# One batch of scores per head pair in a fused state-space and attention kernel: four PSUM banks at once, projections run further ahead, more of the out-projection inside attention

## The chip, the cores and the metric

The kernel runs on one core of a Trainium2 chip. The metric is the device time of one execution in microseconds (us). A core has five engines with a queue each: TensorE (PE in the profile; PEld is its weight load), VectorE (DVE), ScalarE (ACT), GpSimd (POOL) and SyncE (SP), which here issues nearly all DMAs. Matmuls write to PSUM[...].

## What is computed

Two independent parts share one input length T = 2048 and are written side by side. Part A is a diagonal state-space layer; the change leaves it alone. Part B is attention over 64 segments of 32 tokens, each with 8 memory rows in front (32 heads of 128):

```python
for s in range(n_seg):
    h = concat([mem, x[:, s*32:(s+1)*32]])           # 8 + 32 rows
    q, k, v = (einsum('btd,dhe->bhte', h, W) for W in (Wq, Wk, Wv))
    p = softmax(where(mask, q @ k^T * 128**-0.5, -1e9))
    o = einsum('bhte,hed->btd', p @ v, Wo)
    mem = o[:, :8];  outs.append(o[:, 8:])
```

The kernel doesn't follow the recurrence over `mem` one segment after another: it uses a guess of the memory rows for all segments at once, gathers numbers that bound the error, and at the end a flag decides whether a general path must run. In the runs here it isn't run.

## The kernel before

**Stages.** First come the values of part B and part A's scan, then part A's output product (`stage2`), up to about 465 us of the profile. Then follows the stage that the change is about: attention over 16 *head pairs* `hp` (two heads each), from about 465 to 990 us. The last stage is the rest of the out-projection, from 990 us to the end.

**Projections.** `proj` is a generator that makes q and k (transposed) of one head pair in 18 *blocks*: for each of four column quarters q hh0, q hh1, k hh0, k hh1, eight matmuls of 480 columns each (L581), and then two tail blocks (one for q, one for k) of 16 matmuls of 136 columns (L592). Each block accumulates in one of two PSUM banks called P. VectorE copies q blocks and both tails to SBUF (L77, tiles b_q and b_k), ScalarE copies k blocks (L75). In the second quarter ScalarE also squares the weights (`norm`, L564), and the next pair's weights are loaded (`load_wqk`, L554). q and k have two sets of buffers, one per parity of `hp`.

**Units of attention.** A pair has nine units: eight ordinary ones (0 to 7, two blocks of 128 tokens each) and the memory unit, number 8 (`NU`), for the first segment. The order is 0, 1, 2, 3, 4, 5, 8, 6, 7. `att_front` of a unit makes its probabilities, `att_back` uses them two units later:

- Ahead of units 0 and 4, `scores` runs 32 small matmuls (L637), two banks S of 16. They use half of TensorE's columns each, so two of them lie side by side, in 64 rows of the output. ScalarE takes the exponential of each bank (L642, b_e, with a sum in accE). Units 0 to 3 read token columns up to the middle, so these scores need 12 of the pair's 18 blocks; the later ones need all.
- GpSimd multiplies each unit's b_e with the causal mask: two instructions, a *mask pair* (L653, b_mx, four buffers). The memory unit has its own score (L659), exp (L661) and mask (L663, b_ms).
- `att_back` multiplies the masked probabilities with v: four matmuls of 129 columns (L694) into one of two *O pairs* of banks; VectorE adds a memory term (L696, b_s from b_u) and takes reciprocals (L698); GpSimd scales (L702, b_ot). After units 3 and 7 SP writes b_ot to DRAM (b_os, L709 and L710). For the memory unit it is two matmuls (L673), then b_om (L679).

So PSUM holds P, P (projections), S, S (scores and small sums), and O in two pairs.

**The order of the work** on TensorE is written by hand in `kernel_main`: a number of blocks is made ahead of the first unit (`done = 12`), and after each unit blocks are made until `done` is `12 + 2 * (n + 1)`, so two per unit. When the 288 blocks of all pairs are done, each further unit takes two pieces of four matmuls from `early`, a part of the out-projection (`op_some`, L750): tiles 0 and 1, output half 0, three of four head groups, accumulated in the two P banks. A pool framework places semaphores, and a planner orders the instructions of the other engines; each engine's order is then fixed.

**Loads.** b_v and b_u (the values and memory terms of half a pair) have three buffers each; at unit 2 the next pair's first half is loaded, at unit 6 its second (`load_v` L605, `load_u` L618). Four stages of `v_mem` (the values of the memory rows: 32 matmuls L483, DMAs, the certificate term b_ct L498 and its sums L510) go between units 3 to 6 of the first pairs.

**After attention** five transposing loads of b_os (`load_o`, L737, b_ol) are issued on SP. TensorE meanwhile does tiles 2 and 3, half 0 (48 matmuls, banks S), then all four tiles of half 1 (96 matmuls, both O pairs), all with the three head groups that are there. Then the fourth group (64 matmuls), and then tiles 4 to 15. `check` (a generator) loads b_omd transposed (L794), and computes the flag beside tiles 4 to 7.

Of the kernel before, what the change touches and what calls it, by code (L numbers as in the profile page):

```python
# [2 lines left out]

# [6 lines left out]
BF16 = mybir.dt.bfloat16  # L10
I32 = mybir.dt.int32
ACT = mybir.ActivationFunctionType
# [28 lines left out]
UPH = NU + 1  # L41
# [252 lines left out]
class PartB:  # L294
# [219 lines left out]
    def qk_init(self, pool):  # L514
        V, G = self.k.V, self.k.G
        self.qk = []
        for i in range(2):
            self.qk.append([pool.tile([128, 2, QW], BF16, name=f"b_{n}{i}", bufs=1) for n in "qk"])
        self.vmst = []
        for i in range(2):  # L520
            t = pool.tile([128, 4, 128], BF16, name=f"b_vmst{i}", bufs=1)
            V.memset(t[:, :, NM:128], 0.0)
            self.vmst.append(t)
        self.ct = pool.tile([128, 2, 256], BF16, name="b_ct", bufs=1)
        V.memset(self.ct[:], 0.0)
        self.vb, self.ub = [], []
        for i in range(3):
            t = pool.tile([128, NU, VW], BF16, name=f"b_v{i}", bufs=1)
            u = pool.tile([128, NU, VW], BF16, name=f"b_u{i}", bufs=1)
            for c in (0, VW - 1):  # L530
                G.memset(t[:, :, c:c + 1], 1.0)
                G.memset(u[:, :, c:c + 1], float(M))
            self.vb.append(t)
            self.ub.append(u)
        self.vs = pool.tile([128, 2, VW], BF16, name="b_vs", bufs=1)
        G.memset(self.vs[:], 0.0)
        for c in (0, VW - 1):
            G.memset(self.vs[:, :, c:c + 1], 1.0)
        self.ms = []
        self.mx, self.es = [], {}  # L540
        for i in range(4):
            t = pool.tile([128, 4, 128], BF16, name=f"b_mx{i}", bufs=1)
            G.memset(t[:], 0.0)
            self.mx.append(t)
        for i in range(2):
            t = pool.tile([128, 2, 128], BF16, name=f"b_ms{i}", bufs=1)
            G.memset(t[:], 0.0)
            self.ms.append(t)
# [76 lines left out]
        k.SP.dma_start(dst(0, M), self.vt[hb][0:M, :].rearrange("p (h n) -> p h n", h=2))  # L625
        k.SP.dma_start(dst(M, L), self.vx[hb][0:SEG, :].rearrange("p (h n) -> p h n", h=2))

    def scores(self, hp, u0):

        k = self.k  # L630
        qt, kt = self.qk[hp % 2]
        for v in range(2):
            s = k.ps("S")
            for j in range(8):
                g = M + (2 * (u0 + 2 * v + j // 4) + j // 2 % 2) * 128
                for r in (0, 64):
                    k.tc.keep_in_program_order(k.PE.matmul(  # L637
                        s[r:r + 64, j * 64:j * 64 + 64], kt[:, j % 2, g + r:g + r + 64], qt[:, j % 2, g + r:g + r + 64],
                        start=True, stop=True))
            e = self.p3.tile([128, 512], BF16, name="b_e", bufs=3)  # L640
            i = hp * UPH + u0 + v
            k.S.activation(e[:], s[:], ACT.Exp, scale=float(E) ** -0.5, accum_out=self.accE[:, i:i + 1])  # L642
            self.es[u0 + 2 * v], self.es[u0 + 2 * v + 1] = (e[:, 256 * a:256 * a + 256] for a in range(2))

    def att_front(self, hp, u):
        k = self.k; PE = k.PE
        if u < NU:
            if u % 4 == 0:
                self.scores(hp, u)
            m = self.mx[u % 4]  # L650
            e = self.es.pop(u).rearrange("p (j q) -> p j q", j=4)
            for r in (slice(0, 64), slice(64, 128)):
                k.G.tensor_tensor(m[r, :, r], e[r], k.maskX[r, r].unsqueeze(1).to_broadcast([64, 4, 64]), ALU.mult)  # L653
            return m
        qt, kt = self.qk[hp % 2]
        s = k.ps("S")
        i = hp * UPH + u
        for hh in range(2):
            PE.matmul(s[:, hh * L:(hh + 1) * L], kt[:, hh, 0:128], qt[:, hh, 0:L], start=True, stop=True)  # L659
        e = self.p3.tile([128, 2 * L], BF16, name="b_es", bufs=1)  # L660
        k.S.activation(e[:], s[:, 0:2 * L], ACT.Exp, scale=float(E) ** -0.5, accum_out=self.accE[:, i:i + 1])  # L661
        m = self.ms[hp % 2]
        k.G.tensor_tensor(m[:, :, 0:L], e[:].rearrange("p (j q) -> p j q", j=2), k.maskM[:].unsqueeze(1).to_broadcast([128, 2, L]), ALU.mult)  # L663
        return m
# [45 lines left out]
            k.SP.dma_start(os[1024 * half + 128 * (1 - half):1024 * half + 1024, cs].rearrange("(g p) n -> p g n", p=128), ot[:, 1 - half:NU, :])  # L710

    def attention(self):
        units = [(hp, u) for hp in range(HP) for u in (0, 1, 2, 3, 4, 5, NU, 6, 7)]
        pend = []
        for n, (hp, u) in enumerate(units):
            if u == 2:
                self.load_v(2 * hp + 2)
                self.load_u(2 * hp + 2)
            if u == 3 and hp % 2 == 0:
                self.load_vs(hp // 2)  # L720
            if u == 6:
                self.load_v(2 * hp + 3)
                self.load_u(2 * hp + 3)
            pend.append((hp, u, self.att_front(hp, u)))
            if len(pend) > 2:
                self.att_back(*pend.pop(0))
            yield hp, u
        for p in pend:
            self.att_back(*p)
            yield HP, 0  # L730
# [58 lines left out]
    def check(self):  # L789
        k = self.k; V, S, PE = k.V, k.S, k.PE  # L790
        pool = self.p4

        omT = pool.tile([128, H, MT], BF16, name="c_om", bufs=1)
        k.SP.dma_start(omT[:], self.omd[:, :], transpose=True)  # L794
        a = pool.tile([128, H], FP32, name="c_a", bufs=1)
        d = pool.tile([128, H, M], FP32, name="c_d", bufs=1)
        w = pool.tile([128, M], FP32, name="c_w", bufs=1)
# [29 lines left out]
        for i, (acc, limit, op) in enumerate(((self.accE, RANGE, ALU.is_le), (self.rall, RANGE, ALU.is_le), (self.cert, 0.0, ALU.is_ge))):  # L827
            n = acc.shape[1]
# [104 lines left out]
def kernel_main(tc, A_x, A_Lre, A_Lim, A_Bre, A_Bim, A_Cre, A_Cim, A_logdt, A_Dskip, B_x, B_mem0, B_Wq, B_Wk, B_Wv, B_Wo, out,  # L933
                force=False, dbg=None):
    with ExitStack() as ctx:
        k = K(tc, ctx)
# [3 lines left out]
        a = PartA(k, A_x, A_Lre, A_Lim, A_Bre, A_Bim, A_Cre, A_Cim, A_logdt, A_Dskip, out)  # L940
        b = PartB(k, B_x, B_mem0, B_Wq, B_Wk, B_Wv, B_Wo, out)
# [10 lines left out]
        with pool("p1", "right") as p1:  # L952
# [35 lines left out]
            v = values()  # L988
            done = 0
# [16 lines left out]
            for n in range(PC * NB):  # L1006
# [7 lines left out]
                want = 20 + 4 * (n + 1) if n < 4 else 36 + (92 * (n - 3) + 27) // 28  # L1014
# [33 lines left out]
        with pool("p2", "right") as p2:  # L1048
            g = b.guess()
# [15 lines left out]
        with pool("p3", "right") as p3:  # L1065
            b.p3 = p3
            b.qk_init(p3)
            pr, at = b.proj(), b.attention()
            vms = [b.v_mem(hb) for hb in range(HB)]
            for hb in range(2):  # L1070
                next(vms[hb])
            vm = vms[0]
            done = 12
            next(vm)
            b.load_v(0)
            for i in range(done):
                next(pr)
                if i in (0, 2):
                    next(vm)
                if i == 2:  # L1080
                    b.load_u(0)
                    b.load_v(1)
                if i == 5:
                    b.load_u(1)
            b.wo0, b.acc = [], {}
            early = b.op_some([(0, 0), (1, 0)], range(3), "P", 2)
            for n, (hp, u) in enumerate(at):
                if u in (3, 5, 6) and hp < 7:
                    next(vms[hp + 1])
                if u == 4 and hp < 6:  # L1090
                    next(vms[hp + 2])
                if u == 4 and 8 <= hp < 12:
                    w = k.w8((8, 512), "wo0")
                    k.SP.dma_start(w, b.Wo[:, 8 * (hp - 8):8 * (hp - 7), 0:512])
                    b.wo0.append(w)
                if u == 6 and hp in (4, 8, 12):
                    b.load_o(0, hp // 4 - 1)
                want = min(18 * HP, 12 + 2 * (n + 1))
                if done == want:
                    for _ in range(2):  # L1100
                        next(early, None)
                while done < want:
                    next(pr)
                    done += 1
                    if done == 18 * HP:
                        w1 = xep.tile([128, KC, XP], BF16, name="b_xe")
                        b.wo1 = w1[:].rearrange("p c n -> p (c n)")[:, 0:H * 512].rearrange("p (h n) -> p h n", h=H)
                        k.SP.dma_start(b.wo1, b.Wo[:, :, 512:D])
            for _ in early:
                pass  # L1110

        with pool("olb", "right", 5) as olb, pool("p4", "right") as p4:
            b.p4 = p4
            b.olp[1] = olb
            for i in range(5):
                b.load_o(*divmod(i + 3, 4))
            for _ in b.op_some([(2, 0), (3, 0)], range(3), "S"):
                pass
            for _ in b.op_some([(0, 1), (1, 1), (2, 1), (3, 1)], range(3), "O"):
                pass  # L1120
            for half in range(2):
                for t in range(4):
                    b.op(t, half, 3)
                    b.evac(t, half)
            ck = b.check()
            for tb in range(1, 4):
                if tb < 3:
                    for q in range(4):
# [83 lines left out]
```

## Time and profile before

| | us |
|---|---|
| median of 3 runs (1207.6 to 1208.32) | 1207.8 |
| the profiled execution's own time | 1207.88 |
| its span, first to last instruction | 1205.6 |
| TensorE busy (8104 matmuls) | 1198.5 |
| VectorE / ScalarE / GpSimd busy | 585.4 / 350.0 / 355.3 |
| projection matmuls L581 (2048 of 480 columns) | 433.8 |
| scores L637 (1024) | 25.7 |
| values L694 (512) | 51.1 |
| mask pairs L653 (256 instructions) | 170.0 |

TensorE's granted clock is 0.999 of full speed in the profile. Busy time is the union of the shown durations; matmuls overlap in it, since the next one starts before the last has left the array. A row of the timeline gives start, length, engine, line, operation, output<-inputs, shape and number of merged instructions, and in brackets the engine's idle time before it with what ended it. A row of the waits gives the waiting instruction, what it waited for, the total in us, the number of times and the longest.

### The profile page before, as it was taken

Reading aid. Unit: us, or ns where it says so; the run is one execution under the profiler, and the core shown is the slowest. Engines: PE = TensorE matmul, PEld = TensorE weight load, DVE = VectorE, ACT = ScalarE, POOL = GpSimd, SP = SyncE. Lnnn points to the kernel's source line nnn. Section 1 sums busy time; section 2 is a strip of 40 time slices with the busy share of each in tenths; the row PEclk is TensorE's granted clock in tenths of the full one; section 3 lists DMA queues with packets and bytes.
Section 4 is the critical chain, followed back from the end, with each engine's and each line's share of the span. In section 5 each row is a group of like instructions: output and inputs, shape, how many; then the busy total and the mean of one; then the engine's idle time right before and its main releaser. Section 6 shows DMA issues by size and latency. Waiting matters only on the chain.

```text
span 1205.6 us, 19999 instructions
## 1 busy us (share of the span) xinstructions
PE 1198.5 (99%) x8104; PEld 610.1 (51%) x8104; DVE 585.4 (49%) x1004; ACT 350.0 (29%) x713; POOL 355.3 (29%) x484
## 2 busy tenths in 40 slices
PE   9999999999999999999999999999999999999998
PEld 4444444444445544555555555555555554444444
DVE  4889999999973333344444444444444441100000
ACT  3344344443420002433443333333333310000000
POOL 1000000000022332565556665555556670000000
PEclk9999999999999999999999999999999999999999
DMA  9942332331666722999687767565676459507000
GB/s 227 270 132 60 97 97 62 96 99 51 157 179 209 237 79 69 202 245 214 167 190 165 177 167 170 136 134 140 147 171 143 105 179 233 144 18 157 18 25 21
DMA packets 333872, 168.48 MB, mean 140 GB/s; under 512 B 144513, under 2 KB 327609, under 8 KB 333761
## 3 DMA queue, kind: packets, MB, share of 16 engines
q1 hardware_dynamic: 331696, 165.33, 55.4%
q10 hardware_dynamic: 2080, 1.84, 0.5%
q8 instruction: 65, 1.06, 0.4%
q14 instruction: 31, 0.25, 0.1%
HBM read 89.74 MB, written 43.70 MB: 111 GB/s over the span
## 4 chain that ended last, share of the span: by engine, by line
PE 98%; POOL 1%; DMA 0%; issue 0%; DVE 0%; POOLq 0%
PE psP L581 34%; PE psS L750 10%; PE psS L385 9%; PE psP L385 9%; PE psO L233 9%; PE psP L287 5%; PE psS L287 5%; PE psP L750 4%; PE psO L694 3%; PE psP L592 3%; PE psO L750 2%; PE psS L637 2%; PE psS L783 1%; PE psP L483 1%; PE psO L464 1%; POOL b_mx L653 0%
## 5 line engine op out<-in xcount | busy, mean ns | idle before, releaser
L581 PE MATMUL psP<-b_xe,w 128*128 128x480 bf16 x2048 | 433.8, 366 | 0.0
L581 PEld LDWEIGHTS <-w 128*128 128x128 bf16 x2048 | 194.8, 98 | 188.8
L653 POOL TENSOR_TENSOR b_mx<-b_e,maskX 64x256 bf16<-64x256 bf16 x256 | 170.0, 664 | 159.2 <-PE psO L694 86.2
L696 DVE TENSOR_TENSOR b_s<-psO,b_u 128x516 f32<-128x516 f32 x128 | 88.4, 691 | 175.1 <-PE psO L694 137.7
L282 POOL TENSOR_TENSOR a_xd<-a_xn,b_wide 128x512 f32<-128x512 bf16 x32 | 36.9, 1154 | 418.0 <-DMA a_xn<-in_A_x_dram 348.2
L385 PEld LDWEIGHTS <-b_xe 128*128 128x128 bf16 x1024 | 99.7, 98 | 119.1 <-DVE b_xe L77 0.3
L77 DVE CAST b_q<-psP 128x480 bf16<-128x480 f32 (+2 forms) x160 | 92.2, 585 | 119.8 <-PE psP L581 105.4
L750 PEld LDWEIGHTS <-b_ol 128*128 128x128 bf16 x960 | 93.4, 98 | 111.4 <-issue 0.2
L702 POOL TENSOR_TENSOR b_ot<-b_s,b_rall 128x512 bf16<-128x512 f32 x128 | 133.0, 1040 | 54.8 <-DVE b_rall L698 51.5
L75 ACT ACTIVATE b_k<-psP 128x480 bf16<-128x480 f32 x128 | 73.0, 570 | 217.6 <-PE psP L581 213.4
L233 PE MATMUL psO<-w,a_bt 128*128 128x512 bf16 x512 | 115.7, 379 | 0.0
L750 PE MATMUL psS<-w,b_ol 128*128 128x512 bf16 x416 | 92.3, 379 | 0.0
L385 PE MATMUL psS<-w,b_xe 128*128 128x512 bf16 x384 | 90.7, 379 | 0.0
L385 PE MATMUL psP<-w,b_xe 128*128 128x512 bf16 x384 | 90.7, 379 | 0.0
L233 PEld LDWEIGHTS <-a_bt 128*128 128x128 bf16 x512 | 49.7, 98 | 59.0
L287 PEld LDWEIGHTS <-a_hs 128*128 128x128 bf16 x512 | 49.5, 98 | 58.3
L77 DVE CAST b_ost<-psS 128x512 bf16<-128x512 f32 x13 | 9.0, 691 | 138.6 <-PE psS L750 138.6
L564 ACT ACTIVATE b_wide<-w 128x1024 bf16<-128x1024 bf16 x64 | 67.3, 1051 | 7.2 <-POOL b_ct L498 6.7
L75 ACT ACTIVATE b_vst<-psS 128x512 bf16<-128x512 f32 x56 | 33.4, 597 | 98.1 <-PE psS L385 75.7
L287 PE MATMUL psS<-w,a_hs 128*128 128x512 bf16 x256 | 57.9, 379 | 0.0
L287 PE MATMUL psP<-w,a_hs 128*128 128x512 bf16 x256 | 57.9, 379 | 0.0
L75 ACT ACTIVATE b_vst<-psP 128x512 bf16<-128x512 f32 x56 | 33.4, 597 | 82.1 <-PE psP L385 75.9
(202 smaller groups left out, 1107.6 us busy)
## 6 DMA issues: line engine op xcount, KB each, us to landing
b_v<-b_vx SPq DMA_DIRECT2D x32, 512.0 KB
b_u<-b_vt SPq DMA_DIRECT2D x128, 128.0 KB
b_vx<-b_vst SPq DMA_DIRECT2D x56, 256.0 KB
w<-in_B_Wv_dram SPq DMA_DIRECT2D x14, 1024.0 KB
w<-in_B_Wo_dram SPq DMA_DIRECT2D x12, 1024.0 KB
w<-in_B_Wq_dram SPq DMA_DIRECT2D x16, 512.0 KB
w<-in_B_Wk_dram SPq DMA_DIRECT2D x16, 512.0 KB
b_os<-b_ot SPq DMA_DIRECT2D x16, 512.0 KB
```

The source lines that it names most:

```text
L75: self.S.activation(out, in_, ACT.Copy)
L77: self.V.tensor_copy(out, in_)
L233: m = PE.matmul(u[:, i, :], self.bt[:, i, c, :], self.xT[tb][:, c, :], start=(c == 0), stop=(c == KC - 1))
L282: G.tensor_tensor(xd[:], xn[:], dB[:, hs], ALU.mult)
L287: PE.matmul(py[:], self.hs[tb][:, pc, i, tt * 128:(tt + 1) * 128], self.ct[half, i][:, pc, :], start=(pc == 0 and i == 0), stop=(pc == PC ...
L385: m = self.k.PE.matmul(p[:], self.xe[:, c, t * 128:(t + 1) * 128], w[:, c, :], start=(c == 0), stop=(c == KC - 1))
L564: k.tc.keep_in_program_order(k.S.activation(wide, w[:, i * KC:(i + 1) * KC, hh * 128:(hh + 1) * 128], ACT.Square, accum_out=self.nrm[:, n: ...
L581: PE.matmul(p[:, 0:480], w[:, i * KC + c, hh * 128:(hh + 1) * 128], self.xe[:, c, 480 * q:480 * q + 480], start=(c == 0), stop=(c == KC - 1))
L653: k.G.tensor_tensor(m[r, :, r], e[r], k.maskX[r, r].unsqueeze(1).to_broadcast([64, 4, 64]), ALU.mult)
L696: V.tensor_tensor(s[:], o[:, :, 0:VW], ut[:, 2 * v:2 * v + 2, :], ALU.add)
L702: k.G.tensor_tensor(ot[:, 2 * v:2 * v + 2, :].rearrange("p g (h e) -> p g h e", h=2), s[:, :, 1:257].rearrange("p g (h e) -> p g h e", h=2 ...
L750: k.PE.matmul(self.acc[t, half], ol[:, h8, tt * 128:(tt + 1) * 128], self.wo_half(half, h), start=(h == 0), stop=(h == H - 1))
```

## The change

- `scores` runs once per pair, ahead of unit 0: 64 matmuls in a row into four banks, one O pair and both S banks. It needs all 18 blocks of the pair. The four exponentials are put in the program one by one (`exps`): the first at once, two after the next two blocks, the fourth after the third; b_e has four buffers instead of three. (In the order that the planner gives ScalarE, all four stand together.)
- Projections: 19 blocks are made ahead of the first unit instead of 12.
- The order of units is 0, 1, 2, 3, 8, 4, 5, 6, 7; the second load of b_v and b_u goes to unit 5.
- `early` is lengthened by tiles 2 and 3, half 0 (in the S banks), three head groups, and later units of the last pair take three pieces instead of two. The same work is taken out of the stage after attention.
- `check` starts earlier: its load of b_omd is issued behind the first of the five transposing loads.

```diff
-    def scores(self, hp, u0):
+    def scores(self, hp):
         k = self.k
         qt, kt = self.qk[hp % 2]
-        for v in range(2):
-            s = k.ps("S")
+        o = k.ps("O")
+        banks = [o[:, 0, :], o[:, 1, :]] + [k.ps("S")[:] for i in range(2)]
+        for v in range(4):
             for j in range(8):
-                g = M + (2 * (u0 + 2 * v + j // 4) + j // 2 % 2) * 128
+                g = M + (4 * v + j // 2) * 128
                 for r in (0, 64):
                     k.tc.keep_in_program_order(k.PE.matmul(
-                        s[r:r + 64, j * 64:j * 64 + 64], ...
+                        banks[v][r:r + 64, j * 64:j * 64 + 64], ...
-            e = self.p3.tile([128, 512], BF16, name="b_e", bufs=3)
-            i = hp * UPH + u0 + v
-            k.S.activation(e[:], s[:], ACT.Exp, scale=float(E) ** -0.5, accum_out=self.accE[:, i:i + 1])
-            self.es[u0 + 2 * v], self.es[u0 + 2 * v + 1] = (e[:, 256 * a:256 * a + 256] for a in range(2))
+        self.todo = [(hp, v, banks[v]) for v in range(4)]
+        self.exps()
+
+    def exps(self):
+        if self.todo:
+            k = self.k
+            hp, v, s = self.todo.pop(0)
+            e = self.p3.tile([128, 512], BF16, name="b_e", bufs=4)
+            i = hp * UPH + v
+            k.S.activation(e[:], s, ACT.Exp, scale=float(E) ** -0.5, accum_out=self.accE[:, i:i + 1])
+            self.es[2 * v], self.es[2 * v + 1] = (e[:, 256 * a:256 * a + 256] for a in range(2))
...
-            if u % 4 == 0:
-                self.scores(hp, u)
+            if u == 0:
+                self.scores(hp)
...
-        units = [(hp, u) for hp in range(HP) for u in (0, 1, 2, 3, 4, 5, NU, 6, 7)]
+        units = [(hp, u) for hp in range(HP) for u in (0, 1, 2, 3, NU, 4, 5, 6, 7)]
...
-            if u == 6:
+            if u == 5:
                 self.load_v(2 * hp + 3)
                 self.load_u(2 * hp + 3)
...
         k.SP.dma_start(omT[:], self.omd[:, :], transpose=True)
+        yield
...
-            done = 12
+            done = 19
...
-            early = b.op_some([(0, 0), (1, 0)], range(3), "P", 2)
+            early = chain(b.op_some([(0, 0), (1, 0)], range(3), "P", 2), b.op_some([(2, 0), (3, 0)], range(3), "S", 2))
...
-                want = min(18 * HP, 12 + 2 * (n + 1))
+                want = min(18 * HP, 19 + 2 * (n + 1))
                 if done == want:
-                    for _ in range(2):
+                    for _ in range(3 if u > 3 else 2):
                         next(early, None)
+                for _ in range(2 if done == want else 0):
+                    b.exps()
                 while done < want:
                     next(pr)
+                    b.exps()
                     done += 1
...
             b.olp[1] = olb
+            ck = b.check()
             for i in range(5):
                 b.load_o(*divmod(i + 3, 4))
-            for _ in b.op_some([(2, 0), (3, 0)], range(3), "S"):
-                pass
+                if i == 0:
+                    next(ck)
             for _ in b.op_some([(0, 1), (1, 1), (2, 1), (3, 1)], range(3), "O"):
                 pass
...
-            ck = b.check()
```

More of the change, by code (lines that the diff above doesn't have):

```diff
@@ L1 @@
 from contextlib import ExitStack
+from itertools import chain
 import math
@@ L539, in qk_init @@
         self.ms = []
-        self.mx, self.es = [], {}
+        self.mx, self.es, self.todo = [], {}, []
         for i in range(4):
@@ L626, in load_vs @@
         k.SP.dma_start(dst(M, L), self.vx[hb][0:SEG, :].rearrange("p (h n) -> p h n", h=2))
-    def scores(self, hp, u0):
+    def scores(self, hp):
         k = self.k
         qt, kt = self.qk[hp % 2]
-        for v in range(2):
-            s = k.ps("S")
+        o = k.ps("O")
+        banks = [o[:, 0, :], o[:, 1, :]] + [k.ps("S")[:] for i in range(2)]
+        for v in range(4):
             for j in range(8):
-                g = M + (2 * (u0 + 2 * v + j // 4) + j // 2 % 2) * 128
+                g = M + (4 * v + j // 2) * 128
                 for r in (0, 64):
                     k.tc.keep_in_program_order(k.PE.matmul(
-                        s[r:r + 64, j * 64:j * 64 + 64], kt[:, j % 2, g + r:g + r + 64], qt[:, j % 2, g + r:g + r + 64],
+                        banks[v][r:r + 64, j * 64:j * 64 + 64], kt[:, j % 2, g + r:g + r + 64], qt[:, j % 2, g + r:g + r + 64],
                         start=True, stop=True))
-            e = self.p3.tile([128, 512], BF16, name="b_e", bufs=3)
-            i = hp * UPH + u0 + v
-            k.S.activation(e[:], s[:], ACT.Exp, scale=float(E) ** -0.5, accum_out=self.accE[:, i:i + 1])
-            self.es[u0 + 2 * v], self.es[u0 + 2 * v + 1] = (e[:, 256 * a:256 * a + 256] for a in range(2))
+        self.todo = [(hp, v, banks[v]) for v in range(4)]
[8 more added lines that the diff above has]
+            self.es[2 * v], self.es[2 * v + 1] = (e[:, 256 * a:256 * a + 256] for a in range(2))
     def att_front(self, hp, u):
```

## The prediction, made before the changed kernel was run

> **What bounds the kernel now.** I read the page first: busy share by engine, then the chain of waits.
>
> ```profile
> span 1205.6 us, 19999 instructions
> PE 1198.5 (99%) x8104; PEld 610.1 (51%) x8104; DVE 585.4 (49%) x1004; ACT 350.0 (29%) x713; POOL 355.3 (29%) x484
> PE 98%; POOL 1%; DMA 0%; issue 0%; DVE 0%; POOLq 0%
> ```
>
> TensorE is the kernel, and no other engine is near it. So a saving must be TensorE time in which no matmul starts. "Busy" hides such time, because a matmul's shown duration overlaps the next. I therefore compare starts: in the timeline, a row of n matmuls that is W long has its last start at row start + W − one duration (0.366 us for 480 columns, 0.379 for 512, 0.196 for a score). The list of waits names two groups, and the timeline shows both inside head pairs:
>
> ```profile
> PEld L637 <- issue: 12.7, 32, 0.4
> PE psO L673 <- POOL b_ms L663: 0.9, 1, 0.9
> ```
>
> ```profile
> 615.14 0.95 PE L637 MATMUL psS<-b_q,b_k 128*64 128x64 bf16 x32
> 615.25 0.57 ACT L75 ACTIVATE b_k<-psP 128x480 bf16<-128x480 f32 x1 [1.05 <-PE psP L581]
> 616.02 0.41 PE L694 MATMUL psO<-b_v,b_mx 128*128 128x129 bf16 x4
> ...
> 626.38 3.41 PE L581 MATMUL psP<-b_xe,w 128*128 128x480 bf16 x16
> ...
> 629.71 0.70 PE L637 MATMUL psS<-b_q,b_k 128*64 128x64 bf16 x32
> 630.34 0.41 PE L694 MATMUL psO<-b_v,b_mx 128*128 128x129 bf16 x4
> ```
>
> Sixteen projection matmuls start (3.41 − 0.366)/15 = 0.203 us apart. After the last (629.42) another would be due at 629.62; the scores start at 629.71: **0.09 us to enter**. Their last start is 630.21, 16 ns apart, and the values matmul comes at 630.34: **0.11 us to leave**. The 615 batch has the same work but runs 0.95 instead of 0.70: its last matmuls wait for the b_k copy that ends at 615.82. That is the first batch of a head pair, and **the wait of 0.25 us** is in all 16 of them.
>
> The end of attention has one more:
>
> ```profile
> 984.49 1.89 PE L750 MATMUL psP<-w,b_ol 128*128 128x512 bf16 x8
> 985.86 1.04 POOL L702 TENSOR_TENSOR b_ot<-b_s,b_rall 128x512 bf16<-128x512 f32 x1
> 986.86 0.33 POOL L663 TENSOR_TENSOR b_ms<-b_es,maskM 128x80 bf16<-128x80 bf16 x1
> 987.25 0.29 PE L673 MATMUL psO<-b_vs,b_ms 128*128 128x129 bf16 x2 [0.87 <-POOL b_ms L663]
> ```
>
> The next matmul was due at 984.49 + 1.89 − 0.379 + 0.216 = 986.22 and started at 987.25: 1.03 us, because the mask of the memory unit stood behind other GpSimd work.
>
> [...] The scores alone here run with 64 output columns (128*64 in the rows); [...]
>
> **The change, part by part.** All engines execute as many instructions as before; only order, banks and buffers differ.
>
> *One batch for two.* 16 entries and exits go: 16 × 0.20 = 3.2 us. The price could depend on the batch's size, but it is the same in both rows; bounds 0 to 3.8 (the third matmul of each batch is also some 0.03 late).
>
> *Projections ahead.* 19 blocks before the first unit instead of 12. The last columns of q and k are now followed by one block of the next pair, 8 × 0.203 = 1.62 us, before the scores, and only the last four score matmuls (0.95 us later) wait for that copy. VectorE needs 0.22 latency + 0.42 + 0.16 for it: cover 2.5 us, so the 0.25 goes: 16 × 0.25 = 4.0 us. Bounds 0 to 4.0.
>
> *New waits at a pair's start.* Set t = 0 at its first score. TensorE: scores to 1.13 (64 × 16 ns + exit), then per unit a values group (4 × 0.059) and two blocks: units at 1.13, 4.60, 8.08. In ScalarE's new order four exps and two norm squares stand ahead of the next b_k copy. The exps follow each other by 0.57 and the squares by 1.18 (timeline near 630). From 0.55 (977.68 to 978.23 in the trace): exps end 2.8, squares 5.2, copy 5.8. The PSUM bank that it frees is wanted at 6.46: 0.66 us in hand. The O pair lent to the scores is read by the first two exps until 1.8 and wanted at 4.6. So: nothing. If this cover is gone, each 0.1 us costs 1.5 us over 15 pairs.
>
> GpSimd has 2.4 us of work per 3.47 us unit (mask pair 1.43, b_ot 1.04). Masks start 1.3 after the first score (977.68 to 978.99), and unit 0's are wanted at 8.08. The memory unit's mask now stands behind six and a half mask pairs; worked through with its waits it is done at 17.7, wanted at 23: nothing. The memory-value sums come one unit after their b_ct instead of two: b_ct done 19, wanted 26.6.
>
> *SP queue.* [...] The second b_v and b_u load of a pair moves from its eighth unit to its seventh (its buffer is free at the sixth); all b_v and b_u loads are used six units (20 us) or more after issue, and the b_os writes only after the pairs. Weight loads wait for the same freed buffers and keep 14 blocks (some 25 us) before use. The tightest is Wq for pair 1: pair 0's projection now runs without units between, so its next block comes at 465.4 + 16 × 1.62 + 2 × 0.94 = 493 instead of 495.7. Wq and Wk are issued at 480.1 to 484.4; up to 490 the windows move 2.4 MB, and 2.1 MB are ahead or theirs. It fits by some 3 us; if not, it costs 1 to 3 us once, and the first pair's units, which need b_v and b_u, start 10 us later than before with the loads where they were.
>
> *The end.* Three quarters of the out-projection for tiles 2 and 3 (48 × 0.216 = 10.4 us) moves from after attention into it: no time by itself. In the last pair a unit holds only 8 or 12 out-projection matmuls, so TensorE runs faster than GpSimd. TensorE reaches the values of the memory unit after scores 1.13, six values groups 1.42, 4 × 8 + 2 × 12 matmuls 12.1 and the memory score 0.06: at **14.7**. GpSimd, without a gap from 1.3, has six and a half mask pairs (1.43), four b_ot (1.07 with what lies between) and the mask itself (0.33) by then in its order: **15.2**. So a wait of some 0.6 us with the semaphore, instead of 1.03: **0.4 gained**, bounds −1.5 (GpSimd also held up by b_s, 2 us late) to +1.0 (no wait).
>
> After attention the five b_ol transposes take SP 22.07 us from 993.98, that is from 4.3 us after the last values matmul (989.7), and the b_omd transpose (1.23) now follows the first. The first is wanted after 96 matmuls (20.7 us), and is issued by 4.3 + 4.9 = 9.2. The second was wanted after 48 + 96 + 64 matmuls (45 us), now after 96 + 64 (34.6 us), and all five are issued by 4.3 + 22.1 + 1.3 = 28. Nothing. b_omd lands some 16 us earlier, so the VectorE check in front of the b_ost copies isn't late although these come 10.4 us sooner. The big Wo load (issued when the projections end; its traffic stops at about 991, used at 999.9) keeps 24 us of work ahead.
>
> **Sum.** 3.2 + 4.0 + 0.4 = 7.6 us. The profiled execution took 1207.88 (span 1205.6 + 2.3 around it), the median is 1207.8; so **1200.2**, and with some of the 0.03s **1200.0 us**.
>
> **Rivals.** *The wait moves* to the q/k tail copies (VectorE has b_s 0.69, reciprocal 0.18 and a b_q copy 0.66 there: 1.5 of the 2.5 us): 0.25 stays, gain 3.6, 1204.2. The profile speaks against it, since VectorE is at 49%. *Little happens*: [...] the mask of the memory unit or Wq comes later and eats the gain: about 1206. Against it: equal exit times in both batch kinds. *Slower*: ScalarE's block of four exps and two squares holds a projection bank at each pair's start. Past 0.66 us of lateness it costs 15 times the rest; 0.5 us more eats the gain, 0.7 more (copy 1.35 late) gives 1210.5. It decides if the exps wait for their e buffers or space out to 0.59 + 0.20 and the squares to 1.25: that adds 1.0, a 0.35 us wait, 5 us, still faster. The scores not being one batch is excluded by the program's order: 64 in a row.
>
> **How the numbers follow.** As worked out (1198.7 to 1202) 0.83; wait moves 0.10; little 0.04; slower 0.03. Less than 0.2% (2.4 us) can't be told from no change here. Range 1198.7 [...] to 1203.6 (half the gain).
>
> **What would show it.** After: 16 score rows of x64 about 1.2 us long, sixteen "issue" waits instead of 32; no score batch longer than the others; memory-unit wait under 1 us; L694 after scores 0.13 later than the last. Wrong if TensorE waits on ScalarE at the second block of unit 1, on b_ol after attention, or on DMA for pair 1.

## The result, and the profile after

The changed kernel takes 1199.42 us (median of 4 runs, 1198.89 to 1199.58); the kernel before, beside it, 1207.7 (1207.4 to 1208.32). The ratio is 0.993, with a 95% interval of 0.9913 to 0.9947: 8.3 us faster, where 7.8 had been forecast. The profiled executions differ by as much (1207.88 and 1199.58); their spans differ by 7.7. The other 0.6 us lies outside the spans, where no row of the profile shows anything.

Line numbers move with the edit. In the changed kernel L639 are the scores, L652 the exps, L704 the values, L683 the memory unit's values, L673 its mask, L582 and L593 the projections, L76 the b_k copy, L565 the norm squares and L760 the out-projection. The page of the changed kernel (span; busy time of each engine; the chain of waits):

```profile
span 1197.9 us, 20039 instructions
PE 1192.0 (100%) x8104; PEld 608.9 (51%) x8104; DVE 584.8 (49%) x1004; ACT 346.3 (29%) x713; POOL 355.2 (30%) x484
PE 98%; POOL 1%; issue 0%; DVE 0%; ACT 0%; POOLq 0%; ACTq 0%
```

The same 8104 matmuls, the same bound: TensorE is only idle less. The waits of TensorE's weight loads, then of its matmuls (waiting line, what it waited for, total us, times, longest):

```profile
PEld L639 <- issue: 6.0, 15, 0.4
```

```profile
PE psO L683 <- POOL b_ms L673: 0.6, 1, 0.6
```

"Issue" stood at 32 score batches and 12.7 us. Now it is 15 and 6.0: half of the batches are gone (the sixteenth, behind a tail block, has no such row, though by starts it pays the same). The 0.4 us of such a row is the weight load's idle time, not TensorE's loss; that is read from starts. The timeline of TensorE at one pair's start:

```profile
655.70 0.69 PE L639 MATMUL psO<-b_q,b_k 128*64 128x64 bf16 x32
656.23 0.67 PE L639 MATMUL psS<-b_q,b_k 128*64 128x64 bf16 x32
656.84 0.41 PE L704 MATMUL psO<-b_v,b_mx 128*128 128x129 bf16 x4
...
660.32 0.40 PE L704 MATMUL psO<-b_v,b_mx 128*128 128x129 bf16 x4
...
663.79 0.40 PE L704 MATMUL psO<-b_v,b_mx 128*128 128x129 bf16 x4
```

The second half starts 0.53 us after the first: 32 matmuls at 16 ns and 0.02 us that are lost at the third, and no wait. The batch is left once, at 656.84, and the units' values stand 1.14, 4.62 and 8.09 us after the first score; 1.13, 4.60 and 8.08 had been worked out. The end of attention, all engines:

```profile
980.13 1.89 PE L760 MATMUL psS<-w,b_ol 128*128 128x512 bf16 x8
...
982.20 0.33 POOL L673 TENSOR_TENSOR b_ms<-b_es,maskM 128x80 bf16<-128x80 bf16 x1
...
982.58 0.29 PE L683 MATMUL psO<-b_vs,b_ms 128*128 128x129 bf16 x2 [0.56 <-POOL b_ms L673]
```

By starts, the memory unit was due at 980.13 + 1.89 − 0.379 + 0.216 = 981.86 and came at 982.58: 0.72 us lost instead of 1.03.

Over the whole stage, the starts of single matmuls give the sum. Before, every batch lost 0.094 us on entry, 0.020 at its third matmul and 0.112 on exit, 0.226 in all; the first batch of a pair lost 0.25 more. Sixteen batches fewer save 16 × 0.226 = 3.6, sixteen waits less 16 × 0.25 = 4.0, the memory unit 0.3: 7.9. From score to score a pair with memory rows took 32.66 us and takes 32.18, one without 31.57 and 31.09: 0.48 less, which is 0.226 + 0.25. Some 0.3 are lost in the first 10 us, to waits for the loads of part B's input, which have nothing to do with the change: 7.6, and the spans differ by 7.7.

### The profile page after: what moved, and what is told of

The parts are those of the page before. It is cut to its first block, busy times and chain, and to the rows that moved or that the text cites. A ratio compares the mean times of both kernels' runs of the same rounds, so it can differ in the third digit from the quotient of the medians.

```text
span 1197.9 us, 20039 instructions
## 1 busy us (share of the span) xinstructions
PE 1192.0 (100%) x8104; PEld 608.9 (51%) x8104; DVE 584.8 (49%) x1004; ACT 346.3 (29%) x713; POOL 355.2 (30%) x484
## 3 DMA queue, kind: packets, MB, share of 16 engines
q8 instruction: 65, 1.06, 0.4%
## 4 chain that ended last, share of the span: by engine, by line
PE 98%; POOL 1%; issue 0%; DVE 0%; ACT 0%; POOLq 0%; ACTq 0%
PE psP L582 35%; PE psS L760 10%; PE psS L386 9%; PE psP L386 9%; PE psO L234 9%; PE psS L288 5%; PE psP L288 5%; PE psP L760 4%; PE psP L593 3%; PE psO L704 3%; PE psO L760 2%; PE psS L793 1%; PE psO L639 1%; PE psP L484 1%; POOL b_mx L663 1%; PE psS L639 1%
## 5 line engine op out<-in xcount | busy, mean ns | idle before, releaser
L582 PE MATMUL psP<-b_xe,w 128*128 128x480 bf16 x2048 | 435.9, 366 | 0.0
L582 PEld LDWEIGHTS <-w 128*128 128x128 bf16 x2048 | 194.2, 98 | 186.1
L760 PEld LDWEIGHTS <-b_ol 128*128 128x128 bf16 x960 | 93.4, 98 | 110.3
L76 ACT ACTIVATE b_k<-psP 128x480 bf16<-128x480 f32 x128 | 72.7, 568 | 252.3 <-PE psP L582 248.4
L760 PE MATMUL psS<-w,b_ol 128*128 128x512 bf16 x416 | 92.9, 379 | 0.0
L565 ACT ACTIVATE b_wide<-w 128x1024 bf16<-128x1024 bf16 x64 | 67.6, 1056 | 0.5
L76 ACT ACTIVATE b_vst<-psS 128x512 bf16<-128x512 f32 x56 | 33.4, 597 | 96.1 <-PE psS L386 80.3
L76 ACT ACTIVATE b_vst<-psP 128x512 bf16<-128x512 f32 x56 | 33.4, 597 | 83.8 <-PE psP L386 77.7
```

Of the source, the lines that this page charges most:

```text
L76: self.S.activation(out, in_, ACT.Copy)
L565: k.tc.keep_in_program_order(k.S.activation(wide, w[:, i * KC:(i + 1) * KC, hh * 128:(hh + 1) * 128], ACT.Square, accum_out=self.nrm[:, n: ...
L582: PE.matmul(p[:, 0:480], w[:, i * KC + c, hh * 128:(hh + 1) * 128], self.xe[:, c, 480 * q:480 * q + 480], start=(c == 0), stop=(c == KC - 1))
L760: k.PE.matmul(self.acc[t, half], ol[:, h8, tt * 128:(tt + 1) * 128], self.wo_half(half, h), start=(h == 0), stop=(h == H - 1))
```

## The experiments

Three questions stand behind the sum. Is the wait gone because the projections run ahead? Does a batch of scores have a price of its own? And is the moved out-projection really worth nothing? The first three experiments are taken with the kernel before, whose line numbers hold for them. Beside the experiments the kernel before took 1208.0 to 1208.1 us, where it had taken 1207.7 beside the changed kernel, so a difference of medians against 1199.42 is good to some 0.4 us.

**One block further ahead, alone.** If the wait is for the copy of the block just made, one block between is enough.

```diff
-            done = 12
+            done = 13
-                want = min(18 * HP, 12 + 2 * (n + 1))
+                want = min(18 * HP, 13 + 2 * (n + 1))
```

> The kernel before, with its projection blocks one further ahead (13 where it had 12) and nothing else changed: 32 score batches over two banks each are kept. Theory: the first batch of a pair waited 0.25 us for the copies of the last projection block's tail, and a block placed between the tail and the batch covers that wait whole. Then the time falls by 15 to 16 waits of 0.25 us, 3.8 to 4.0 us, to about 1203.8, and the 0.22 us gaps before the first batch of a pair are gone while each of the 32 batches keeps its entry of 0.09 us and its exit of 0.11 us. Rival (all of the change's gain is the switch into and out of the 64-row matmuls): no difference, 1207.8.

(The block whose copy is waited for is an ordinary k block here, ScalarE's, and not the tail; the argument is the same.) Measured: 1211.25 us, ratio 1.0028 (1.0017 to 1.0039). Slower, as neither theory had it. The waits of TensorE's matmuls, and then its timeline and those of ScalarE and GpSimd, show why:

```profile
PE psP L581 <- ACT b_k L75: 6.6, 7, 1.0
```

```profile
645.23 1.78 PE L581 MATMUL psP<-b_xe,w 128*128 128x480 bf16 x8 [0.94 <-ACT b_k L75]
```

```profile
639.28 0.39 ACT L496 ACTIVATE b_wide<-b_vmst 128x248 f32<-128x248 bf16 x1
643.58 1.06 ACT L564 ACTIVATE b_wide<-w 128x1024 bf16<-128x1024 bf16 x1 [3.90 <-POOL b_ct L498]
...
644.63 0.55 ACT L75 ACTIVATE b_k<-psP 128x480 bf16<-128x480 f32 x1
```

```profile
642.84 0.71 POOL L498 TENSOR_TENSOR b_ct<-b_wide 128x248 bf16<-128x248 f32 x1
```

The wait at the scores did go, in every pair: where no memory rows are made, a pair takes 31.32 us from score to score instead of 31.57. But seven pairs have the memory rows' certificate between, and there a norm square (L564) stands behind L495 and L496. All three write the scratch b_wide, which GpSimd has still to read for b_ct. The kernel before has such waits too, but short ones, and TensorE waited for none of them:

```profile
ACT b_wide L564 <- POOL b_ct L498: 6.7, 7, 1.0
```

In the shifted order b_ct comes later behind L496 (3.6 us instead of 0.6) and the b_k copy stands straight behind the square. ScalarE stands for 3.90 us, the b_k copy is late, and the projection's next bank comes free 1.11 us (by starts) after TensorE wants it. 7 × 1.11 − 16 × 0.25 = +3.8; the spans differ by 3.7.

**The same, with scratch of their own** for L495 and L496:

```diff
-        a, b = (self.wide[:, 4 * n * i:4 * n * i + 4 * n].rearrange("p (h n) -> p h n", h=4) for i in range(2))
+        a, b = (self.sq[:, 4 * n * i:4 * n * i + 4 * n].rearrange("p (h n) -> p h n", h=4) for i in (hb % 2, 2))
...
+        self.sq = pool.tile([128, 12 * (NSEG - 2)], BF16, name="b_sq", bufs=1)
```

> The kernel before with 13 blocks ahead, and with scratch of their own for the memory rows' two squares (L495, L496: in bf16 instead of fp32, so the number that bounds the error is rounded more coarsely), where before they shared b_wide with the norm squares. Theory: with 13 ahead, a norm square (L564) waited for GpSimd to read b_wide (b_ct), the b_k copy behind it came late, and TensorE waited 1.11 us in 7 pairs; with separate scratch nothing is to be waited for, and the time is that of the wait theory for 13 blocks, 1203.9. Rival (ScalarE's copies are late because of the squares' place in its order or their length, not because of the shared scratch): TensorE's wait stays, 1209 to 1211.

Measured: 1204.12 us, ratio 0.9966 (0.9953 to 0.9978). TensorE's wait for L75 is gone from its list, the pairs take 32.41 and 31.32 us instead of 32.66 and 31.57, and the gain is 3.9 where 16 × 0.25 = 4.0 was expected. So the wait is shown to be one for a copy, and one block covers it. The loss of the experiment above went with the shared scratch, as its trace had said. (The planner also ordered ScalarE's squares differently here: none stands behind L495 and L496 ahead of a b_k copy. Scratch and order changed together, and the run doesn't part them.)

**All seven blocks, alone.** The projection part of the change in the kernel before:

```diff
-            done = 12
+            done = 19
-                want = min(18 * HP, 12 + 2 * (n + 1))
+                want = min(18 * HP, 19 + 2 * (n + 1))
```

> The projection part of the change alone: the kernel before with 19 blocks ahead of the first unit instead of 12; two batches of two score banks per pair, the old order of units and the old out-projection stay. Theory: the wait of 0.25 us in the first batch of each pair goes and no other comes, since in ScalarE's order of this kernel the four norm squares of a pair stand ahead of the memory rows' writes to b_wide (L495, L496) and none stands behind them with a b_k copy in its tow, as it does with 13 ahead: 15 to 16 times 0.25, so 1203.9. Rival (any distance other than 12 brings ScalarE's wait for b_ct, as 13 did in the pairs with memory rows): 1211.

Measured: 1209.51 us, ratio 1.0013 (1.0007 to 1.002). A miss of 5.6 us, though the theory of the pairs held: they take 32.41 and 31.32 us, and ScalarE doesn't wait. The loss is in the last pair. Its timeline (TensorE, GpSimd's row for the mask), and a table of stretches (TensorE, its weight loads, the other engines' busy us, then the granted clock, the DMA share and GB/s):

```profile
989.31 0.40 PE L673 MATMUL psO<-b_vs,b_ms 128*128 128x129 bf16 x2 [4.28 <-POOL b_ms L663]
```

```profile
988.92 0.33 POOL L663 TENSOR_TENSOR b_ms<-b_es,maskM 128x80 bf16<-128x80 bf16 x1
```

```profile
984.00:989.40 5.40, 1.12 (x9) 0.51 (x10) 1.03 (x3) 0.00 (x0) 5.13 (x8) 0.91 0.08 24
988.50:989.30 0.80, 0.00 (x0) 0.00 (x0) 0.00 (x0) 0.00 (x0) 0.80 (x3) 0.50 0.00 0
989.40:992.00 2.60, 2.60 (x11) 1.30 (x12) 1.08 (x4) 0.00 (x0) 1.85 (x2) 0.50 0.65 201
992.00:995.10 3.10, 2.88 (x11) 1.38 (x11) 2.44 (x8) 0.00 (x0) 1.42 (x2) 0.50 0.01 1
995.10:998.00 2.90, 2.90 (x15) 1.31 (x14) 0.75 (x1) 0.00 (x0) 0.89 (x1) 0.97 0.32 103
```

Seven blocks made earlier are 7 × 1.62 = 11.4 us of TensorE's work that no longer stand between the last pair's units. GpSimd's work per unit stays, so TensorE overtakes it: by starts it waits 4.44 us for b_ms (before 1.03) and 0.68 for a b_mx. And the granted clock changes in this run: the trace's record of it goes to half at 988.46 us, still inside the pause, and back to full at 995.28: 6.83 us, 5.97 of them with work, in which 512-column matmuls start 427 ns apart instead of 216. That costs 2.9 us more. −4.0 + 3.4 + 0.7 + 2.9 = +3.0; at the start of the kernel this run happens to lose 0.4 less to loads, and the spans differ by 2.5. The half clock takes 0.003 off the mean clock of the profiled run (0.997). The means of this kernel's 21 runs lie between 0.996 and 0.999, and their times between 1208.65 and 1211.18 us, so it seems that the slow stretch isn't equally long in all; only one was profiled.

The part of the change that seemed to be worth nothing is thus what pays for the other: 48 out-projection matmuls (10.4 us) fill what the seven blocks leave.

**The changed kernel without that fill.**

```diff
-            early = chain(b.op_some([(0, 0), (1, 0)], range(3), "P", 2), b.op_some([(2, 0), (3, 0)], range(3), "S", 2))
+            early = b.op_some([(0, 0), (1, 0)], range(3), "P", 2)
...
+            for _ in b.op_some([(2, 0), (3, 0)], range(3), "S"):
+                pass
```

> The changed kernel with the out-projection that it took into the last pair of attention (row tiles 2 and 3, first half) put back behind attention, into the score banks. The work is the same. Theory: as cover it is worth time: without it TensorE reaches the last memory unit and the last units' values about 2 us before GpSimd's masks are done, so about 4 us are lost, 1203.4, and the trace shows waits for b_ms and b_mx in the last pair. Rival (moved work has no price of its own and the waits are covered without it): 1199.4.

Measured: 1202.6 us, ratio to the kernel before 0.9954 (0.9941 to 0.9968), so 3.2 slower than the changed kernel. The waits of TensorE's matmuls:

```profile
PE psO L683 <- POOL b_ms L673: 2.3, 1, 2.3
...
PE psO L704 <- POOL b_mx L663: 0.7, 1, 0.7
```

By starts 2.48 for b_ms (0.72 with the fill) and 0.89 for b_mx: 2.65 of the 2.7 us between the spans. The granted clock is 1.00 in each of the stretches that hold these waits (980 to 984 and 984 to 987 us). The memory unit stands two units earlier here than in the experiment above, which is likely why the wait is shorter; that order wasn't tried by itself.

**Two batches in the changed kernel.** The four blocks are issued two and two, with one values group between:

```diff
             if len(pend) > 2:
                 self.att_back(*pend.pop(0))
+            if u == 0:
+                self.score_mm(hp, (2, 3))
             yield hp, u
```

> The changed kernel with its score blocks issued two and two, with the unit's four values matmuls between the two halves; all else stays, the projection distance included. Theory: TensorE pays for each entry into the 64-row matmuls and each exit (0.09 + 0.11 us, and 0.03 at the third matmul), so one more of each in 15 to 16 pairs costs 3.0 to 3.8 us: about 1202.8. ScalarE's exps of the second half start some 0.6 us later, which has to stay covered. Rival (the price goes with the number of matmuls, not of batches): no difference, 1199.4.

Measured: 1202.85 us, ratio to before 0.9957 (0.9943 to 0.997): 3.4 more than the changed kernel. Its timeline (L648 are the scores, L711 the values):

```profile
625.02 0.41 PE L711 MATMUL psO<-b_v,b_mx 128*128 128x129 bf16 x4
625.36 0.69 PE L648 MATMUL psS<-b_q,b_k 128*64 128x64 bf16 x32
625.99 3.41 PE L582 MATMUL psP<-b_xe,w 128*128 128x480 bf16 x16
```

The values end at 625.02 + 4 × 0.059 = 625.26, the second half enters at 625.36 (0.10), has its last start at 625.36 + 0.69 − 0.196 = 625.85, and is left at 625.99 (some 0.13, of which 0.016 is a score's own). A pair takes 32.41 and 31.32 us instead of 32.18 and 31.09: 0.226 × 15 = 3.4. The price is the batch's, be it of 32 or of 64 matmuls.

**Tail straight before the scores,** in the changed kernel, by 18 blocks instead of 19:

```diff
-            done = 19
+            done = 18
-                want = min(18 * HP, 19 + 2 * (n + 1))
+                want = min(18 * HP, 18 + 2 * (n + 1))
```

> The changed kernel with its projection 18 blocks ahead instead of 21, so that a pair's tail columns are again finished straight before its score batch. Theory: in the batch of four blocks the q and k blocks that the tail finishes are wanted late enough that the batch itself covers the copies, as the last pair (which has no block between) shows no wait: no difference, about 1199.4. Rival (the distance of the projection is what removed the wait): 15 waits of 0.25 us come back, about 1203.2.

(The 21 in it counts the two blocks of the first unit; in `done` it is 19.) Measured: 1199.07 us, against 1199.42. No wait came back, as the timeline of TensorE, with VectorE's copy of the tail of k, shows:

```profile
651.37 2.06 PE L593 MATMUL psP<-b_xe,w 128*128 128x136 bf16 x32
653.36 0.69 PE L639 MATMUL psO<-b_q,b_k 128*64 128x64 bf16 x32
653.46 0.51 DVE L78 CAST b_k<-psP 128x256 bf16<-128x256 f32 x2 [0.44 <-PE psP L593]
```

The copy ends at 653.97, 0.61 us after the first score. The tail's columns are wanted by the last four of the 64 matmuls only, 0.95 us after the first: that covers the copy by itself. What the pair needs is all 18 of its blocks, not the nineteenth. (No "issue" row is left for the scores in this run, though by starts each batch still loses 0.094 us on entry: these rows don't measure the price.)

**The same, with the banks in the order 3, 2, 1, 0,** so that the tail's columns are wanted early:

```diff
-        for v in range(4):
+        for v in (3, 2, 1, 0):
```

> The changed kernel with its projection 18 blocks ahead, so that the tail is finished straight before the batch, and with the batch's blocks issued in the order 3, 2, 1, 0, so that its 13th matmul already reads a block that the tail has finished. Theory: a batch of four covers the tail's copies only by the order of its matmuls; wanted so early, the copies are late by 0.45 to 0.6 us in 15 pairs, 7 to 9 us, about 1207. Rival (the copies are done by then, or the wait of the kernel before was no wait for the copies): no difference, 1199.4.

Measured: 1203.91 us, 4.5 more than the changed kernel: neither number. The reason is in its timeline:

```profile
622.74 0.38 PE L639 MATMUL psS<-b_q,b_k 128*64 128x64 bf16 x12
623.05 0.58 PE L582 MATMUL psP<-b_xe,w 128*128 128x480 bf16 x2
623.55 0.51 PE L639 MATMUL psS<-b_q,b_k 128*64 128x64 bf16 x20
```

TensorE's order isn't wholly the program's: only the scores are pinned among themselves, and two projection matmuls have been put into the batch, presumably where the planner saw a wait. They fill it, but they split the batch into 12 and 52: one more exit (0.112) and entry (0.094), in all sixteen pairs. A pair takes 32.40 us instead of 32.18, 0.22 × 16 = 3.5, and the memory unit's wait is 1.66 instead of 0.72: some 4.5, with 4.3 between the spans. So this run says nothing on how late the copies would be, but it prices the switch a second time.

**The slower rival, forced.** One norm square more per pair, written twice to the same place:

```diff
-                            self.norm(hp, w, i, hh)
+                            for _ in range(2 if i == 0 and hh == 0 else 1):
+                                self.norm(hp, w, i, hh)
```

> The changed kernel with one more ScalarE square per pair: the sum of squares of one head of q is formed twice into the same place, ahead of ScalarE's copy of the second projection bank. Theory: that copy is ready only 0.5 to 0.6 us before TensorE wants the bank for its next projection block, so 1.07 to 1.18 us more of ScalarE's work shows as a wait of TensorE of 0.5 to 0.7 us in 15 to 16 pairs: 8 to 11 us, about 1209, and the trace shows the projection's first matmul in the second unit of a pair waiting for ScalarE's copy. Rival (ScalarE is busy 29% of the time, the square is hidden): no difference, 1199.4.

Measured: 1208.56 us, ratio to before 1.0003 (0.9994 to 1.0011): one 1.06 us instruction per pair on an engine that is 29% busy eats the whole gain. The waits of TensorE's matmuls (the line numbers are one higher from the scores on):

```profile
PE psP L582 <- ACT b_k L76: 6.9, 14, 0.5
```

By starts, fourteen waits of 0.653 = 9.1 us, and the medians differ by 9.1. The squares follow each other by 1.18 us, so 1.18 − 0.65 = 0.53 us were in hand.

**A better deal of the pieces.** More out-projection before the last memory unit, less behind it, nothing added; then the same with 18 blocks:

```diff
-                    for _ in range(3 if u > 3 else 2):
+                    for _ in range(1 if u in (0, 7) and n > 139 else 3 if u > 1 else 2):
```

> The changed kernel with the out-projection pieces that stand in the last pair dealt out differently: more of them before the last memory unit and fewer after it, none added. Theory: TensorE reaches the last memory unit later, so the 0.7 us wait for GpSimd's b_ms mask there goes: 1198.7, unless the last units, which have fewer pieces now, wait for b_mx instead. Rival (it only moves the wait to those units): 1199.4.

> The changed kernel with both edits that did not cost: 18 blocks ahead instead of 19, and the out-projection pieces of the last pair dealt out so that more stand before the memory unit. Theory: no wait at the scores and none for b_ms, so 1198.3 to 1198.8. Rival (with 18 ahead the projection ends later, the last units have fewer pieces in front of them and wait for b_mx): 1199 to 1200.

Measured: 1198.73 us (1198.42 to 1198.84), ratio to before 0.9921 (0.9907 to 0.9934), and 1198.72 us (1198.27 to 1198.92) with 18 blocks. In both no wait for b_ms or b_mx is left, and the timeline of the first has the memory unit's values behind an out-projection row and without a bracket:

```profile
980.70 2.75 PE L760 MATMUL psS<-w,b_ol 128*128 128x512 bf16 x12
983.29 0.28 PE L683 MATMUL psO<-b_vs,b_ms 128*128 128x129 bf16 x2
```

They start where they were due: 980.70 + 2.75 − 0.379 + 0.216 = 983.29. That is the 0.7 us of the changed kernel's wait. Both medians lie below those of the changed kernel and of the run at 18 blocks; the gain over these is too small for the bound of 0.2%, and rests on the trace.

## Why the prediction was right

- *One batch for two*: 3.2 forecast, with 0.03 per batch on top; 3.6 measured with it, since it was 0.02. The price per batch held in the split batches (0.22 to 0.23 per pair).
- *Projections ahead*: 4.0 forecast, 4.0 measured; with own scratch it gave 3.9 by itself. The reason given was half of it: the block in between isn't needed, since the order of the 64 matmuls covers the tail's copy, which ends 0.61 us after the first score.
- *Memory unit*: TensorE was expected there 14.7 us after the pair's first score and came at 14.69. The mask was expected done at 15.2 and was at 15.36, because GpSimd began 1.57 and not 1.3 after that score. So the wait was 0.72 instead of 0.6, the gain 0.3 instead of 0.4.
- *ScalarE at a pair's start* is the step that was nearest to failing. The exps were expected from 0.55 and began at 0.80: the first waits for both banks of the O pair, 32 matmuls. The rows of ScalarE after the scores at 655.70:

```profile
656.50 0.60 ACT L652 ACTIVATE b_e<-psO 128x512 bf16<-128x512 f32 x1 [3.87 <-PE psO L639]
...
659.99 1.06 ACT L565 ACTIVATE b_wide<-w 128x1024 bf16<-128x1024 bf16 x1
...
661.04 0.55 ACT L76 ACTIVATE b_k<-psP 128x480 bf16<-128x480 f32 x1
```

The copy ends 5.89 us after the first score (5.8 expected) and the bank is wanted at 6.47. The forced rival put 0.53 us in hand, semaphore included, where 0.66 had been worked out, and showed that lateness costs what it was said to: nearly all of it, in nearly every pair.
- *No time from the moved out-projection by itself* was right as a sum and wrong as a reading. It has no price, but without it 2.7 us more of waits come (3.2 us by the medians). The hand count of the last pair had the moved work in (4 × 8 + 2 × 12 matmuls ahead of the memory unit); the text didn't say that the projections' gain hangs on it.
- *The end*: TensorE waits for no transposing load behind attention, as worked out.
- *The sum* is closer than its terms, by luck: they came to 7.9 by starts where 7.6 was forecast, and chance waits for loads at the start took 0.3 back. The 0.6 us outside the spans are in no term.

The new order of the units, the earlier second load of b_v and b_u and the earlier load of b_omd weren't tried by themselves; what each is worth stays open.

Of the rivals, *the wait moves* fell with the changed kernel's trace, where no batch waits inside, and again with the run at 18 blocks. *Little happens* fell with the result. *Slower* was a true mechanism with half a microsecond between it and the kernel. The mishap that no rival named is that of the first experiment: a scratch shared by two users on ScalarE, which a shift by one block turned into a wait of 3.90 us with the b_k copy behind it.

## What to carry to other kernels

When TensorE is the bound, read starts, not busy time: here the switch into the half-width score matmuls and back cost 0.226 us per batch, of 32 or of 64 alike, so make the batches few. The work moved ahead of its consumer left a hole where it stood, and in the stage's last round something had to fill it (2.7 us more of waits without the fill); count each engine's work per unit there. And before moving work by a block, look on every engine for what shares a buffer with it or with its neighbours, not only at who consumes it: in the first experiment ScalarE stood for 3.90 us over such a buffer, and the b_k copy came late.

## What the runs showed of the hardware

- Entering the half-width score matmuls (128*64 in the rows) cost TensorE 0.094 us and leaving them 0.112, in batches of 32 in the kernel before and of 64 in the changed one. With one batch more per pair, split as 32 and 32 or as 12 and 52, a pair took 0.23 or 0.22 us longer.
- In the one profiled run with 19 blocks ahead in the kernel before, TensorE waited 4.44 us, and the granted clock was 0.50 from 988.46 us, inside the wait, to 995.28, with work in 5.97 of these 6.83 us. Matmuls of 512 columns started 427 ns apart there instead of 216, which cost 2.9 us beyond the wait. In the changed kernel without the fill it waited 2.48 us, and the granted clock was 1.00 there. What sets the clock these runs don't show.
